# Soft-routing weights finished in one pass after attention, and three of five token tiles of each head's output normalised by ScalarE instead of VectorE

## Chip, cores and metric

One core of a Trainium2 chip. The metric is the device time of one execution in microseconds (us). The engines are TensorE (PE, matrix products; PEld is its weight load, which overlaps the products), VectorE (DVE), ScalarE (ACT), GpSimd (POOL) and SyncE (SP), which here only issues DMA transfers. Each engine runs its own instructions in the order in which they were written; semaphores order the engines among each other.

## What is computed

Three layers behind each other, in fp32: attention with a window of 128 tokens and a slope per head, a soft mixture of experts, and a feed-forward layer.

```python
scores = scale * q @ k.T                        # 4 batches x 8 heads, 576 tokens, 64 columns
scores = where(mask, scores + bias, -1e9); scores -= scores.max(-1)
attn = exp(scores); attn /= attn.sum(-1) + 1e-9
x = attn @ v                                    # 2304 tokens x 512
logits = x @ phi                                # 2304 x 32 slots
d = exp(logits - logits.max(0)); d /= d.sum(0) + 1e-9
slot_in = d.T @ x                               # 32 x 512
slot_out[e] = relu(slot_in[e] @ w1[e]) @ w2[e]  # 8 experts, 4 slots each
c = exp(logits - logits.max(1)); c /= c.sum(1) + 1e-9
y = c @ slot_out
h = y @ w_in; out = max(0.01 * h, h) @ w_out
```

Two softmaxes run over the same logits: d over the tokens (to fill the slots), and c, the combine softmax, over the 32 slots of each token.

## The kernel before

**Stages.** Attention over 32 heads g (batch g // 8), then the experts (w1, w2), then the feed-forward layer. In attention each step of a head is a small function; `UNITS` names them and `XO` gives each an offset, and step nm of head g stands at g + XO[nm]. All steps are sorted by that number and written out in that order, so a stretch of one unit holds one step of each kind, of up to five different heads. Each engine's order is what falls to it from this one list.

**A head's steps** that matter here. TQ and TK transpose Q and K (L262). HQ and HK are casts on ScalarE of the upper part of Q and K, two instructions each (L275: the Q cast writes qb, the K cast kb). LQ and LK leave the rest to kq on VectorE (L280, L282). A, B, C are scores for the row maxima (L302, into the PSUM tile sm, of which there are two), XA, XB, XC take the maxima on VectorE (L312, into mn). M transposes mn (L321), MS copies it on ScalarE (L326) and DM sends it by DMA into a row of qb (L329). S and s are the scores proper (L343, L344, the latter needs that row), E0 and E1 the exp on ScalarE (L351), G0 and G1 the masks on GpSimd, P and Q the products with V (L408) into one PSUM tile, o_ps, that all heads share. Its 65th column is the row sum. N1 adds 1e-9 (L423), N2 takes the reciprocal (L425), N3 multiplies (L429), all on VectorE, and N3 writes the head's 64 columns of xs for all five token tiles (4 of 128 tokens, one of 64). The next head's P may write o_ps only when N3 has read it.

```python
          "s": -0.3557, "E0": -0.2345, "E1": 0.1505, "G0": 0.8774, "G1": 0.979, "P": 1.0817,
          "Q": 1.1478, "N1": 1.3456, "N2": 1.5564, "N3": 1.8652}
```

N3 of head g (g + 1.8652) is followed by HQ of head g + 5 (g + 5 - 3.0925 = g + 1.9075).

**A batch's steps** (`batch_parts`, offsets in `YO`) are strewn among the heads of the next batch: transposes of xs (L452, L463) and their copies by ScalarE (L456, L466), logits (L474, added up by L495 and L502), the logits transposed (L509, L510) and copied by ScalarE to lsb (L514, L515), the maximum over the tokens (pm L519 to L523, bm L526, bmv L530, bmx L534, bt L537, btv L544), exp against it (dxv L571, dxa L578), the slots' input (sl L598, L601) and sums (ds, dsv). The combine softmax of a batch runs beside these on VectorE: maximum (tm2 L554), subtraction (tm3 L557), exp on ScalarE (tme L560), sum (cb L581), 1e-9 (cb2), reciprocal (cb3), product (cb4 L590), over the 160 logits that a partition has (5 tiles x 32 slots), into cn. For the last batch these stand in a list of their own behind attention (`TAIL`, `AFTER`).

**Behind attention** TensorE multiplies the slots' input by w1 (L823); ScalarE's Relu (L832) needs the reciprocal of the slots' sums (L828, L829). GpSimd splits cn into two fp32r parts (`csplit`, L848, L849), batches 0 and 1 before the products with w2 (L875), and TensorE transposes them (L855) after the second of these products' steps.

**Between engines on PSUM**: the framework orders any two accesses of different engines to one PSUM tile.

Of the kernel before, what the change touches and what calls it, by code (L numbers as in the profile page):

```python
# [21 lines left out]
def attn_softmoe_ffn(ctx: ExitStack, tc: tile.TileContext, q, k, v, phi, w1, w2, w_in, w_out, cst_in, out):  # L22
# [97 lines left out]
    with tc.manual_schedule():  # L120
# [22 lines left out]
        pmb = view("L", 128, 208)  # L143
        bm4 = at.tile([128, 4, 16], F32, name="bm4")
        lsb = at.tile([128, 5, NS], F32, name="lsb")
# [64 lines left out]
        nc.vector.memset(lsb[64:128, 4, :], NEG)  # L210
# [207 lines left out]
        def norm(i):  # L418
            def f(g):
# [4 lines left out]
                elif i == 1:  # L424
                    nc.vector.reciprocal(rss[g], rss[g])  # L425
                else:
                    r = rss.pop(g).unsqueeze(2)
                    for t in (slice(0, 5),) if g < NG - 1 else (slice(0, 2), slice(2, 5)):
                        nc.vector.tensor_tensor(  # L429
                            out=xs[(g // 4) % 3][:, t, g % 4 * D:g % 4 * D + D], in0=o_ps[:, t, 0:D],  # L430
                            in1=r[:, t].to_broadcast([128, t.stop - t.start, D]), op=ALU.mult)
            return f

        def batch_parts(b):
# [77 lines left out]
            def lnc():  # L512
                p = ts["ln"].rearrange("p (t s) -> p t s", t=5)
                nc.scalar.copy(out=lsb[:, 0:4, :], in_=p[:, 0:4, :])  # L514
                nc.scalar.copy(out=lsb[0:64, 4, :], in_=p[0:64, 4, :])  # L515

            def pm():
                m = small.tile([128, 1], F32, tag="pm", name="pm", bufs=1)
                nc.vector.reduce_max(out=m, in_=ts["lg"] if last else L, axis=AX.X)  # L519
                if b == 0:  # L520
                    nc.vector.tensor_copy(pmb, m.to_broadcast([128, 128]))
                else:
                    nc.vector.tensor_scalar(out=pmb, in0=m.to_broadcast([128, 128]), scalar1=mrun[(b + 1) % 2], scalar2=None, op0=ALU.max)  # L523
# [607 lines left out]
```

## Time and profile before

| | |
|---|---|
| median of 3 runs | 444.44 us (443.29 to 444.61) |
| the profiled execution | 444.21 us, its span 442.5 us |
| TensorE busy, weight loads | 427.3 us (97%), 338.4 us (76%) |
| VectorE busy | 282.9 us (64%) |
| ScalarE busy | 241.1 us (54%) |
| GpSimd busy | 119.9 us (27%) |
| attention | to about 169 us of the span |
| TensorE's granted clock | full in all 40 slices |

Busy time of TensorE counts products whose ends are modelled and which overlap, so a busy TensorE isn't one at its peak. The shares are means over stages: in attention VectorE is nearly always busy, later it is not. A step that an engine does off the chain that sets the pace costs nothing.

### The profile page before, as it was taken

Reading aid. Unit: us, or ns where it says so; the run is one execution under the profiler, and the core shown is the slowest. Engines: PE = TensorE matmul, PEld = TensorE weight load, DVE = VectorE, ACT = ScalarE, POOL = GpSimd, SP = SyncE. Lnnn points to the kernel's source line nnn. Section 1 sums busy time; section 2 is a strip of 40 time slices with the busy share of each in tenths; the row PEclk is TensorE's granted clock in tenths of the full one; section 3 lists DMA queues with packets and bytes.
Section 4 is the critical chain, followed back from the end, with each engine's and each line's share of the span. In section 5 each row is a group of like instructions: output and inputs, shape, how many; then the busy total and the mean of one; then the engine's idle time right before and its main releaser. Section 6 shows DMA issues by size and latency. Waiting matters only on the chain.

```text
span 442.5 us, 9856 instructions
## 1 busy us (share of the span) xinstructions
PE 427.3 (97%) x3490; PEld 338.4 (76%) x3490; DVE 282.9 (64%) x892; ACT 241.1 (54%) x558; POOL 119.9 (27%) x296
## 2 busy tenths in 40 slices
PE   8899998999999999999999999999999999999996
PEld 7798887788788876333776888778878888888884
DVE  5999999899999954112999776767552233225241
ACT  4587776677678733121885755555554345333330
POOL 3377667476666844020000002020202000000000
PEclk9999999999999999999999999999999999999999
DMA  7379887888978879899987005000000003003011
GB/s 168 107 227 245 227 234 218 250 219 246 237 208 232 238 222 374 291 407 412 411 293 252 7 1 190 2 1 0 1 0 0 1 0 144 0 0 145 0 73 72
DMA packets 66834, 70.30 MB, mean 159 GB/s; under 512 B 23168, under 2 KB 42016, under 8 KB 66784
## 3 DMA queue, kind: packets, MB, share of 16 engines
q1 hardware_dynamic: 66640, 69.53, 49.9%
q8 instruction: 28, 0.46, 0.5%
q14 instruction: 22, 0.18, 0.1%
q10 hardware_dynamic: 144, 0.13, 0.1%
HBM read 64.85 MB, written 4.72 MB: 157 GB/s over the span
## 4 chain that ended last, share of the span: by engine, by line
PE 85%; DVE 5%; ACT 4%; DMA 3%; issue 2%; POOL 1%; DVEq 0%; SPq 0%; ACTq 0%; POOLq 0%
PE acc L994 44%; PE o_ps L408 5%; PE sm L302 4%; PE ph L971 3%; PE st L344 3%; PE st L343 3%; DMA qb<-ms 3%; PE pb L875 3%; PE pb L823 3%; PE tp L262 3%; PE o_ps L152 2%; PE tp L452 1%; ACT kb L275 1%; PE tp L474 1%; PE tp L598 1%
## 5 line engine op out<-in xcount | busy, mean ns | idle before, releaser
L994 PE MATMUL acc<-p,p 128*128 128x512 f32 x648 | 161.3, 394 | 0.0
L994 PEld LDWEIGHTS acc<-p,p 128*128 128x128 f32 x648 | 120.3, 188 | 26.9 <-issue 2.6
L984 DVE TENSOR_TENSOR p<-ar,p 128x384 fp32r<-128x384 f32 x96 | 53.2, 556 | 92.5 <-ACT ar L980 92.3
L976 ACT ACTIVATE p<-ph 128x384 fp32r<-128x384 f32 (+1 forms) x97 | 47.5, 490 | 94.5 <-PE ph L971 94.5
L312 DVE CUSTOM_DVE_ANT_0 junk<-sm,ar 128x256 bf16<-128x256 f32 (+2 forms) x160 | 53.5, 375 | 3.0 <-PE sm L302 2.5
L994 PE MATMUL acc<-b,p 128*128 128x512 f32 x216 | 54.3, 395 | 0.0
L351 ACT ACTIVATE ar<-st 128x512 f32<-128x512 f32 x64 | 38.4, 599 | 19.2 <-PE st L344 10.4
L994 PEld LDWEIGHTS acc<-b,p 128*128 128x128 f32 x216 | 39.9, 188 | 9.8 <-issue 1.5
L980 ACT ACTIVATE ar<-ph 128x384 f32<-128x384 f32 x96 | 47.0, 489 | 0.0
L769 POOL TENSOR_TENSOR p<-ar,p 128x512 fp32r<-128x512 f32 x8 | 10.4, 1295 | 128.1 <-ACT p L769 111.4
L343 PE MATMUL st<-kq 128*128 128x256 f32 (+1 forms) x160 | 40.0, 278 | 0.0
L408 PE MATMUL o_ps<-ar 128*64 128x65 f32 x992 | 39.1, 225 | 0.0
L344 PE MATMUL st<-qb,kb 128*128 128x256 f32 (+1 forms) x160 | 36.0, 272 | 2.4 <-DMA qb<-ms 2.3
L302 PE MATMUL sm<-kb,qb 96*128 96x256 f32 (+2 forms) x160 | 34.9, 312 | 3.4 <-DVE mn L312 1.4
L408 PEld LDWEIGHTS o_ps<-ar 128*64 128x64 f32 x992 | 34.8, 138 | 4.0 <-issue 1.2
L275 ACT ACTIVATE qb<-tp 64x288 fp32r<-64x288 f32 x64 | 27.8, 434 | 9.4 <-PE tp L262 8.2
L280 DVE SCALAR_TENSOR_TENSOR kq<-tp,qb 64x288 fp32r<-64x288 f32 x64 | 29.2, 457 | 4.5 <-ACT qb L275 2.6
L971 PE MATMUL ph<-p,p 128*128 128x384 f32 x96 | 32.0, 339 | 0.0
L288 POOL TENSOR_SCALAR_AFFINE_SELECT kq<-qb 64x576 fp32r<-64x576 f32 x32 | 21.2, 662 | 37.6 <-ACT qb L275 30.6
L344 PEld LDWEIGHTS st<-qb,kb 128*128 128x128 f32 (+1 forms) x160 | 28.5, 178 | 3.6 <-DMA qb<-ms 3.5
L275 ACT ACTIVATE kb<-tp 64x288 fp32r<-64x288 f32 x64 | 27.9, 437 | 6.0 <-PE tp L262 4.6
L282 DVE TENSOR_TENSOR kq<-tp,kb 64x288 fp32r<-64x288 f32 x64 | 29.1, 455 | 1.8 <-ACT kb L275 0.2
(195 smaller groups left out, 610.4 us busy)
## 6 DMA issues: line engine op xcount, KB each, us to landing
p<-in_moe_w_dram SPq DMA_DIRECT2D x56, 256.0 KB, 4.6
p<-in_moe_w_dram SPq DMA_DIRECT2D x7, 1024.0 KB, 10.2
p<-in_moe_w_in_dram SPq DMA_DIRECT2D x5, 1024.0 KB, 5.2
p<-in_moe_w_out_dram SPq DMA_DIRECT2D x5, 1024.0 KB, 14.5
ar<-in_k_dram SPq DMA_DIRECT2D x32, 144.0 KB, 3.8
ar<-in_q_dram SPq DMA_DIRECT2D x32, 144.0 KB, 3.4
out_dram<-ar SPq DMA_DIRECT2D x17, 256.0 KB, 2.2
ar<-in_v_dram SPq DMA_DIRECT2D x32, 128.0 KB, 4.2
```

The source lines that it names most:

```text
L275: nc.scalar.activation(out=b1, in_=pr, func=AF.Copy, scale=2.0 ** (g % H - 2) if half else 1.0)
L302: nc.tensor.matmul(sl, lhsT=Q1[0:MROW, 128 * t:128 * t + mr], rhs=K1[0:MROW, c0:c1], start=True, stop=True)
L312: nc.vector.tensor_tensor_reduce(out=jk[0:mr, 0:n], in0=sl, in1=maskt[0:mr, m0:m0 + n], op0=ALU.add, op1=ALU.max, accum_out=mn[g % 2][0:mr ...
L343: nc.tensor.matmul(sl, lhsT=KX[:, k0:k1], rhs=QA[:, q0:q1], start=True, stop=False)
L344: nc.tensor.matmul(sl, lhsT=kb[g % R][:, k0:k1], rhs=qb[g % R][:, q0:q1], start=False, stop=True)
L351: nc.scalar.activation(out=e, in_=sts.pop((g, s)), func=AF.Exp, scale=2.0 ** -(g % H + 1))
L408: nc.tensor.matmul(o_ps[64 * u:64 * u + 64, t, :], lhsT=lt, rhs=r, start=st, stop=sp, tile_position=(0, 64 * u))
L971: nc.tensor.matmul(p, lhsT=mst[:, 128 * f:128 * f + 128], rhs=rhs, start=True, stop=True)
L976: nc.scalar.activation(out=G[t0, f][0][:, c], in_=H1[t0, f][:, c], func=AF.Prelu, alpha=0.01)
L980: nc.scalar.activation(out=gg, in_=H1.pop((t0, f)), func=AF.Prelu, alpha=0.01)
L984: nc.vector.tensor_tensor(out=g2, in0=G0.pop((t0, f)), in1=g1.bitcast(F32), op=ALU.subtract)
L994: nc.tensor.matmul(acc[t0][t], lhsT=(g1, g1, g2)[k][:, 128 * t:128 * t + 128], rhs=(WO1, WO2, WO1)[k][c][:, i], start=(f == f0 and k == 0) ...
```

## The change

Two things. The combine softmax leaves the batches' steps: lsb is gone, the logits are copied straight to cn, and one pass over all four batches (640 logits a partition, 20 rows of 32) follows attention, ahead of the experts' products: maximum, subtraction, exp, sum, 1e-9, reciprocal, product. And N3 does only token tiles 0 and 1 on VectorE (128 columns a partition); tiles 2, 3 and 4 are three activations on ScalarE, Copy with the reciprocal as a scale per partition, 64 columns each. The last head is as before. With it, the maximum over tokens isn't widened to 128 and 96 columns any more: the transpose reads it through a broadcast view, and the second transpose becomes four matmuls of two columns in four column groups of TensorE. No offset of a head's steps changes.

```diff
--- before
+++ after
@@ -140,9 +139,8 @@
-        pmb = view("L", 128, 208)
+        cmx = view("L", 5 * B, 208)
-        lsb = at.tile([128, 5, NS], F32, name="lsb")
@@ -207,7 +205,7 @@
-        nc.vector.memset(lsb[64:128, 4, :], NEG)
+        nc.vector.memset(cn[64:128, :, 4, :], NEG)
@@ -424,11 +422,13 @@
                 elif i == 1:
                     nc.vector.reciprocal(rss[g], rss[g])
                 else:
-                    r = rss.pop(g).unsqueeze(2)
-                    for t in (slice(0, 5),) if g < NG - 1 else (slice(0, 2), slice(2, 5)):
-                        nc.vector.tensor_tensor(
-                            out=xs[(g // 4) % 3][:, t, g % 4 * D:g % 4 * D + D], in0=o_ps[:, t, 0:D],
-                            in1=r[:, t].to_broadcast([128, t.stop - t.start, D]), op=ALU.mult)
+                    r = rss.pop(g)
+                    x = xs[(g // 4) % 3][:, :, g % 4 * D:g % 4 * D + D]
+                    for t in (slice(0, 2),) if g < NG - 1 else (slice(0, 2), slice(2, 5)):
+                        nc.vector.tensor_tensor(out=x[:, t], in0=o_ps[:, t, 0:D],
+                                                in1=r[:, t].unsqueeze(2).to_broadcast([128, t.stop - t.start, D]), op=ALU.mult)
+                    for t in (2, 3, 4) if g < NG - 1 else ():
+                        nc.scalar.activation(out=x[:, t], in_=o_ps[:, t, 0:D], func=AF.Copy, scale=r[:, t:t + 1])
             return f
 
         def batch_parts(b):
@@ -511,36 +511,32 @@
 
             def lnc():
                 p = ts["ln"].rearrange("p (t s) -> p t s", t=5)
-                nc.scalar.copy(out=lsb[:, 0:4, :], in_=p[:, 0:4, :])
-                nc.scalar.copy(out=lsb[0:64, 4, :], in_=p[0:64, 4, :])
+                nc.scalar.copy(out=cn[:, b, 0:4, :], in_=p[:, 0:4, :])
+                nc.scalar.copy(out=cn[0:64, b, 4, :], in_=p[0:64, 4, :])
 
             def pm():
-                m = small.tile([128, 1], F32, tag="pm", name="pm", bufs=1)
+                st["pm"] = m = small.tile([128, 1], F32, tag="pm", name="pm", bufs=1)
                 nc.vector.reduce_max(out=m, in_=ts["lg"] if last else L, axis=AX.X)
-                if b == 0:
-                    nc.vector.tensor_copy(pmb, m.to_broadcast([128, 128]))
-                else:
-                    nc.vector.tensor_scalar(out=pmb, in0=m.to_broadcast([128, 128]), scalar1=mrun[(b + 1) % 2], scalar2=None, op0=ALU.max)
+                if b > 0:
+                    nc.vector.tensor_tensor(out=m, in0=m, in1=mrun[(b + 1) % 2], op=ALU.max)
 
             def bm():
-                nc.tensor.transpose(tp("bm", [128, 128]), pmb, ident)
+                nc.tensor.transpose(tp("bm", [128, 128]), st["pm"].to_broadcast([128, 128]), ident)
 
             def bmv():
-                st["mx"] = mx = small.tile([128, 4, NS], F32, tag="mx", name="mx", bufs=1)
-                nc.vector.reduce_max(out=mx[:, 0, :], in_=ts.pop("bm").rearrange("p (j s) -> p s j", j=4), axis=AX.X)
-
-            def bmx():
-                mx = st["mx"]
-                nc.vector.tensor_copy(mx[:, 1:4, :], mx[:, 0:1, :].to_broadcast([128, 3, NS]))
+                st["mx"] = mx = small.tile([128, 4 * NS], F32, tag="mx", name="mx", bufs=1)[:, 0:NS]
+                nc.vector.reduce_max(out=mx, in_=ts.pop("bm").rearrange("p (j s) -> p s j", j=4), axis=AX.X)
 
             def bt():
-                nc.tensor.transpose(tp("bt", [128, 128]), st["mx"].rearrange("p a s -> p (a s)"), ident)
+                p = tp("bt", [128, 2])
+                for t in range(4):
+                    nc.tensor.matmul(p[32 * t:32 * t + 32, :], lhsT=st["mx"], rhs=ident[:, 0:2], start=True, stop=True, tile_position=(0, 32 * t))
 
             def btv():
                 mo, mw = mrun[(b + 1) % 2], mrun[b % 2]
                 p = ts.pop("bt")
                 if b > 0:
-                    st["al"] = al = small.tile([128, 1], F32, tag="al", name="al", bufs=1)
+                    st["al"] = al = small.tile([128, 16], F32, tag="al", name="al", bufs=1)[:, 0:1]
                     nc.vector.tensor_tensor(out=al, in0=mo, in1=p[:, 0:1], op=ALU.subtract)
                 if not last:
                     nc.vector.tensor_copy(mw, p[:, 0:1])
@@ -548,16 +544,6 @@
             def bta():
                 if b > 0:
                     nc.scalar.activation(out=st["al"], in_=st["al"], func=AF.Exp)
-
-            def tm2():
-                st["cm"] = m = small.tile([128, 5], F32, tag="cm", name="cm", bufs=1)
-                nc.vector.reduce_max(out=m, in_=lsb, axis=AX.X)
-
-            def tm3():
-                nc.vector.tensor_tensor(out=cn[:, b], in0=lsb, in1=st["cm"].unsqueeze(2).to_broadcast([128, 5, NS]), op=ALU.subtract)
-
-            def tme():
-                nc.scalar.activation(out=cn[:, b], in_=cn[:, b], func=AF.Exp)
 
             dq = [(slice(0, 128), slice(0, 4)), (slice(0, 64), slice(4, 5))]
 
@@ -566,9 +552,9 @@
-                        nc.vector.tensor_tensor(out=dn[r, t], in0=p[r, t], in1=st["mx"][r, 0:1, :].to_broadcast([r.stop, t.stop - t.start, NS]), op=ALU.subtract)
+                        nc.vector.tensor_tensor(out=dn[r, t], in0=p[r, t], in1=st["mx"][r].unsqueeze(1).to_broadcast([r.stop, t.stop - t.start, NS]), op=ALU.subtract)
-                    nc.vector.tensor_tensor(out=dn, in0=lsb, in1=st["mx"][:, 0:1, :].to_broadcast([128, 5, NS]), op=ALU.subtract)
+                    nc.vector.tensor_tensor(out=dn, in0=cn[:, b], in1=st["mx"].unsqueeze(1).to_broadcast([128, 5, NS]), op=ALU.subtract)
@@ -576,18 +562,6 @@
                         nc.scalar.activation(out=st["dn"][r, t], in_=st["dn"][r, t], func=AF.Exp)
                 else:
                     nc.scalar.activation(out=st["dn"], in_=st["dn"], func=AF.Exp)
-
-            def cb():
-                nc.vector.reduce_sum(out=st["cm"], in_=cn[:, b], axis=AX.X)
-
-            def cb2():
-                nc.vector.tensor_scalar(out=st["cm"], in0=st["cm"], scalar1=1e-9, scalar2=None, op0=ALU.add)
-
-            def cb3():
-                nc.vector.reciprocal(st["cm"], st["cm"])
-
-            def cb4():
-                nc.vector.tensor_tensor(out=cn[:, b], in0=cn[:, b], in1=st["cm"].unsqueeze(2).to_broadcast([128, 5, NS]), op=ALU.mult)
 
             def sl():
                 p, dn = tp("sl", [128, 512], "st"), st["dn"]
...
@@ -794,8 +763,15 @@
             for i in range(n):
                 nc.tensor.matmul(t[:, 0:128], lhsT=ident, rhs=ident, start=True, stop=True)
 
-        for k in AFTER:
-            after[k]()
+        cf = cn.rearrange("p b t s -> p (b t) s")
+        cmb = cmx.unsqueeze(2).to_broadcast([128, 5 * B, NS])
+        nc.vector.reduce_max(out=cmx, in_=cf, axis=AX.X)
+        nc.vector.tensor_tensor(out=cf, in0=cf, in1=cmb, op=ALU.subtract)
+        nc.scalar.activation(out=cf, in_=cf, func=AF.Exp)
+        nc.vector.reduce_sum(out=cmx, in_=cf, axis=AX.X)
+        nc.vector.tensor_scalar(out=cmx, in0=cmx, scalar1=1e-9, scalar2=None, op0=ALU.add)
+        nc.vector.reciprocal(cmx, cmx)
+        nc.vector.tensor_tensor(out=cf, in0=cf, in1=cmb, op=ALU.mult)
         he, so = ar[:, x0:x0 + F], ar[:, x0 + F:x0 + F + DM]
 
         def to_hT(h):
```

The order in which ScalarE does its work, before, from the sum of the logits' first half (L495) over the next two heads (kb, qb: casts of K and Q of a head; st: scores; ms: maxima; tp: a transpose in PSUM):

```order
L495 COPY ar<-tp 128x144
L275 ACTIVATE kb_88<-tp 64x288 x2
L351 ACTIVATE ar<-st 128x512
L326 CAST ms<-tp 5x128
L456 COPY ar<-tp 128x4x128
L351 ACTIVATE ar<-st 128x512
L275 ACTIVATE qb_92<-tp 64x288 x2
L275 ACTIVATE kb_91<-tp 64x288 x2
```

And in the changed kernel, the same place:

```order
L495 COPY ar<-tp 128x144
L273 ACTIVATE kb_88<-tp 64x288 x2
L349 ACTIVATE ar<-st 128x512
L324 CAST ms<-tp 5x128
L456 COPY ar<-tp 128x4x128
L349 ACTIVATE ar<-st 128x512
L431 ACTIVATE ar<-o_ps,rs 128x64 x3
L273 ACTIVATE qb_92<-tp 64x288 x2
L273 ACTIVATE kb_91<-tp 64x288 x2
```

The three activations (L431) stand between the exp and the next Q cast; so they do in every head, but for one in eight in which a copy of a transpose (L456) comes between them and the cast. The first of them waits for VectorE's piece of the same normalisation, which stands ahead of it in the program.

VectorE's order, before, in the head that holds the middle of a batch's steps (dn: exponents of the slots' softmax; mx: maxima over tokens; cm: the combine softmax's rows; rs: row sums):

```order
L280 SCALAR_TENSOR_TENSOR kq_96<-tp,qb_95 64x288 x2
L571 TENSOR_TENSOR dn<-lsb,mx 128x160
L534 COPY mx<-mx 128x96
L282 TENSOR_TENSOR kq_96<-tp,kb_94 64x288 x2
L423 TENSOR_SCALAR rs<-o_ps 128x5
L312 ISA junk,mn_99<-sm,ar 64x192
L312 ISA mn_99 64x1
L425 RECIPROCAL rs<-rs 128x5
L554 TENSOR_REDUCE cm<-lsb 128x5
L557 TENSOR_TENSOR cn<-lsb,cm 128x160
L544 TENSOR_TENSOR al<-col,tp 128x1
L546 COPY col<-tp 128x1
```

And in the changed kernel:

```order
L557 TENSOR_TENSOR dn<-cn,mx 128x160
L280 TENSOR_TENSOR kq_96<-tp,kb_94 64x288 x2
L421 TENSOR_SCALAR rs<-o_ps 128x5
L310 ISA junk,mn_99<-sm,ar 64x192
L310 ISA mn_99 64x1
L423 RECIPROCAL rs<-rs 128x5
L540 TENSOR_TENSOR al<-col,tp 128x1
L542 COPY col<-tp 128x1
L428 TENSOR_TENSOR ar<-o_ps,rs 128x2x64
```

The widening copy and the two steps of the combine softmax are gone from between the rest of K and the normalisation, and that is two token tiles wide.

VectorE's order at the end of attention in the changed kernel (col: the slots' sums; pa: a product in PSUM), where before the same steps were 160 wide and of the last batch alone:

```order
L598 TENSOR_TENSOR col<-col,tp 32x1
L768 TENSOR_REDUCE ar<-cn 128x20
L769 TENSOR_TENSOR cn<-cn,ar 128x640
L771 TENSOR_REDUCE ar<-cn 128x20
L772 TENSOR_SCALAR ar<-ar 128x20
L773 RECIPROCAL ar<-ar 128x20
L774 TENSOR_TENSOR cn<-cn,ar 128x640
L804 TENSOR_SCALAR col<-pa 128x1
L805 RECIPROCAL col<-col 128x1
```

The reciprocal for the Relu (L804, L805) stands behind the whole pass.

## Rows read from the trace of the kernel before

**Rows 1.** Busy time of each engine in a stretch of attention (count), clock, DMA.
```profile
30.00:150.00 120.00, 115.37 (x1584) 99.75 (x1583) 112.35 (x467) 86.33 (x208) 78.94 (x206) 1.00 0.86 233
```
**Rows 2.** TensorE's waits in 30 to 150: in total, times, longest.
```profile
PEld sm L302 <- ACT kb L275: 3.7, 12, 0.4
PEld st L344 <- DMA qb<-ms: 3.5, 5, 1.7
...
PEld sm L302 <- DVE mn L312: 1.2, 4, 0.6
```
**Rows 3.** Timeline of ScalarE: start, duration, what, [idle before and its releaser].
```profile
90.89 0.88 ACT L275 ACTIVATE kb<-tp 64x288 fp32r<-64x288 f32 x2
...
93.34 0.59 ACT L456 COPY ar<-tp 128x512 f32<-128x512 f32 x1 [0.81 <-PE tp L452]
93.82 0.60 ACT L351 ACTIVATE ar<-st 128x512 f32<-128x512 f32 x1
94.31 0.89 ACT L275 ACTIVATE qb<-tp 64x288 fp32r<-64x288 f32 x2
95.22 0.89 ACT L275 ACTIVATE kb<-tp 64x288 fp32r<-64x288 f32 x2
...
98.10 0.91 ACT L275 ACTIVATE qb<-tp 64x288 fp32r<-64x288 f32 x2 [0.19 <-PE tp L262]
```
**Rows 4.** Timeline of VectorE in the same heads.
```profile
95.58 0.94 DVE L280 SCALAR_TENSOR_TENSOR kq<-tp,qb 64x288 fp32r<-64x288 f32 x2
96.56 0.94 DVE L282 TENSOR_TENSOR kq<-tp,kb 64x288 fp32r<-64x288 f32 x2
...
98.09 0.49 DVE L429 TENSOR_TENSOR ar<-o_ps,rs 128x320 f32<-128x320 f32 x1
...
99.86 0.94 DVE L280 SCALAR_TENSOR_TENSOR kq<-tp,qb 64x288 fp32r<-64x288 f32 x2
```
**Rows 5.** L429, the normalisation: ns shortest/median/longest, first and last start, shapes.
```profile
L429 DVE TENSOR_TENSOR ar<-o_ps,rs x31: 472/490/493, 26.8 to 167.2; 128x320 f32<-128x320 f32 x31
L429 DVE TENSOR_TENSOR ar<-ol,rs x2: 291/318/345, 168.8 to 169.0; 128x128 f32<-128x128 f32 x1, 128x192 f32<-128x192 f32 x1
```
**Rows 6.** Timeline of ScalarE: two neighbouring copies of different width.
```profile
108.33 0.27 ACT L514 COPY lsb<-tp 128x128 f32<-128x128 f32 x1
108.49 0.18 ACT L515 COPY lsb<-tp 64x32 f32<-64x32 f32 x1
```
**Rows 7.** Timeline of ScalarE: the first Relu of the experts.
```profile
184.44 0.69 ACT L832 ACTIVATE ar<-pb,col 128x512 f32<-128x512 f32 x1 [6.69 <-PE pb L823]
```
**Rows 8.** Timeline at the tail: a copy of the logits and its wait.
```profile
171.48 0.28 ACT L500 COPY ar<-tp 128x144 f32<-128x144 f32 x1 [0.88 <-DVE pm L519]
```
**Rows 9.** Timeline of ScalarE: casts and a copy of the other heads.
```profile
86.12 0.88 ACT L275 ACTIVATE kb<-tp 64x288 fp32r<-64x288 f32 x2
...
89.81 0.43 ACT L275 ACTIVATE qb<-tp 64x288 fp32r<-64x288 f32 x1 [1.01 <-PE tp L262]
...
102.80 0.59 ACT L456 COPY ar<-tp 128x512 f32<-128x512 f32 x1 [0.67 <-PE tp L452]
...
107.41 0.89 ACT L275 ACTIVATE qb<-tp 64x288 fp32r<-64x288 f32 x2 [0.18 <-PE tp L262]
...
111.61 0.88 ACT L275 ACTIVATE qb<-tp 64x288 fp32r<-64x288 f32 x2 [0.29 <-PE tp L262]
...
119.28 0.88 ACT L275 ACTIVATE kb<-tp 64x288 fp32r<-64x288 f32 x2 [1.74 <-PE tp L262]
...
123.75 0.88 ACT L275 ACTIVATE qb<-tp 64x288 fp32r<-64x288 f32 x2
```
**Rows 10.** Busy time of what touches cm, 30 to 168: VectorE (count), clock, DMA.
```profile
30.00:168.00 138.00, 5.67 (x18) 1.00 0.84 233
```
**Rows 11.** Timeline behind attention: VectorE's reduction, GpSimd's first split after transposes.
```profile
176.72 0.30 DVE L554 TENSOR_REDUCE cm<-lsb 128x5 f32<-128x160 f32 x1
...
194.54 0.32 POOL L848 CAST ar<-cn 128x160 fp32r<-128x160 f32 x1 [17.55 <-PE pa L855]
```

More of the change, by code (lines that the diff above doesn't have):

```diff
@@ L48, in attn_softmoe_ffn @@
           "xs": 9.4718, "xsc": 9.7691, "lh": 10.0639, "lgc": 10.0708, "pm": 10.6372, "lx": 10.7576,
-          "bm": 11.6027, "bmv": 11.8446, "ln": 10.8721, "lnc": 10.9955, "bmx": 12.1976, "dxv": 12.0436,
+          "bm": 11.6027, "bmv": 11.8446, "ln": 10.8721, "lnc": 10.9955, "dxv": 12.0436,
           "dxa": 12.5969, "bt": 12.663, "btv": 12.7744, "bta": 12.9593, "sl": 12.8123, "slv": 13.1223,
-          "ds": 13.3756, "dsv": 13.7379, "tm2": 12.6955, "tme": 13.0753, "cb": 13.9763, "tm3": 12.7455,
-          "cb2": 13.9963, "cb3": 14.0163, "cb4": 14.0363}
+          "ds": 13.3756, "dsv": 13.7379}
     ZA = {"DQK": 0.8, "DV": 1.2, "W0": 0.3, "EARLY": 0.8, "L0": 3.0, "L1": 4.0,
@@ L624, in dsv @@
                 nc.vector.tensor_tensor(out=ssum[0:NS], in0=ssum[0:NS], in1=p[0:NS, 2:3], op=ALU.add)
-            F.update(lgc=lgc, lx=lx, ln=ln, lnc=lnc, pm=pm, bm=bm, bmv=bmv, bmx=bmx, bt=bt, btv=btv, bta=bta, tm2=tm2, tme=tme,
-                     dxv=dxv, dxa=dxa, tm3=tm3, cb=cb, cb2=cb2, cb3=cb3, cb4=cb4, sl=sl, slv=slv, ds=ds, dsv=dsv)
+            F.update(lgc=lgc, lx=lx, ln=ln, lnc=lnc, pm=pm, bm=bm, bmv=bmv, bt=bt, btv=btv, bta=bta,
+                     dxv=dxv, dxa=dxa, sl=sl, slv=slv, ds=ds, dsv=dsv)
             return F
@@ L633, in attn_softmoe_ffn @@
                  "G0": mask(0), "G1": mask(1), "P": attend(0), "Q": attend(1), "N1": norm(0), "N2": norm(1), "N3": norm(2)}
-        TAIL = ["xt3", "xt5", "xt4", "xt3c", "xt5c", "xt4c", "lh", "pm", "lgc", "lx", "bm", "ln", "bmv", "dxv", "dxa", "bmx", "bt", "sl",
-                "btv", "bta", "lnc", "slv", "ds", "dsv", "tm2", "tm3"]
+        TAIL = ["xt3", "xt5", "xt4", "xt3c", "xt5c", "xt4c", "lh", "pm", "lgc", "lx", "bm", "ln", "bmv", "dxv", "dxa", "bt", "sl",
+                "btv", "bta", "lnc", "slv", "ds", "dsv"]
         TAIL = [(B - 1, nm) for nm in TAIL]
-        AFTER = [(B - 1, nm) for nm in ("tme", "cb", "cb2", "cb3", "cb4")]
         LAST = {"xt2": 5.07, "xs": 5.1, "xt2c": 5.3, "xsc": 5.31, "li": 6.3}
         FILL = dict(zip(("xt4", "lh", "ln", "bt", "ds"), WN[2:]))
-        after = {}
         ev = []
@@ L646, in attn_softmoe_ffn @@
             for nm, f in batch_parts(b).items():
-                if (b, nm) in AFTER:
-                    after[b, nm] = f
-                    continue
                 if (b, nm) in TAIL:
```

## The prediction

> **What bounds the kernel now.** I read the busy times of the attention stage first, then what TensorE waited for there, then the engines' timelines head by head, and last the start of the expert stage. Between 30 and 150 us TensorE is busy 115.37 of 120 us and VectorE 112.35, while ScalarE has 86.33 [rows 1]. So TensorE stands idle for 4.63 us at most, and whatever makes VectorE lighter can return no more than that in this stretch; ScalarE looks as if it had 33 us to give away. The waits say otherwise: TensorE's weight loads for the row-max scores (L302) waited for the K cast of ScalarE (L275) 12 times, 3.7 us, for the row of maxima coming by DMA 3.5 us, and for VectorE's maxima only 1.2 us [rows 2]. ScalarE has idle time, but not where TensorE waits for it.
>
> The timeline shows the tie. In one head the K cast ends at 91.77, TensorE then does scores and a transpose, ScalarE copies that transpose at 93.34 after a wait of 0.81 us for it, and from there runs without a gap: exp at 93.82, Q cast at 94.31, K cast at 95.22 until 96.11 [rows 3]. That is a closed ring of 4.34 us (K cast, TensorE, copy, exp, Q cast, K cast); anything put between exp and Q cast lengthens it. VectorE has a ring of its own in these heads: its rest of Q starts at 95.58 and again at 99.86, 4.28 us with no gap [rows 4].
>
> **The change, part by part.**
>
> *VectorE's share of the normalisation.* It falls from 320 columns a partition (490 ns) to 128; the last head has such a piece, 291 ns [rows 5]. That is 0.20 us off VectorE in 30 heads, 6 us of VectorE's time. None of it shortens a ring that I found closed on TensorE; it helps where TensorE waits for maxima, and the bound on that is the 1.2 us of [rows 2]. I credit the whole 1.2.
>
> *ScalarE's share.* Three activations of 64 columns with a scale per partition. Nothing like it is in the trace. A 64x32 copy takes 0.18 us and a 128x128 one 0.27, and the second of them starts 0.16 after the first, so neighbours overlap by 0.11 [rows 6]; 64 columns lie at some 0.21. A Relu with a scale per partition takes 0.69 at 512 columns [rows 7], against 0.60 for an exp with a plain scale [rows 3]: 0.09 for the scale. One is 0.30 then, three in a row hold the engine 3 x (0.30 - 0.11) = 0.57, say 0.6. Below: the scale's 0.09 vanishes in the overlap, 3 x 0.10 = 0.3. Above: no overlap, as the two halves of a Q cast show none (0.89 for the two [rows 3], 0.43 for one [rows 9]), 3 x 0.30 = 0.9. I take 0.6, by the overlapping rows, since these are neighbours with separate columns.
> By itself: the Trainium skill, page "ScalarE: Activation LUTs", section "What ACT_TABLE_LOAD costs", gives 186 ns + 0.833 ns per column, 93 ns more for a pointer operand, and an overlap of 93 ns; that would be some 0.72 us for the three (an estimate), and by it the time below would be about 2 us more. The same page's rules for kernel authors put multiplications on VectorE rather than ScalarE.
>
> *When they may start.* The built order puts the three after the exp and ahead of the next Q cast, and the Q cast can't pass them. They need the reciprocal, and they also come behind VectorE's piece: both read one PSUM tile, and the trace shows that two engines that only read one are kept apart, for ScalarE's copy at 171.48 waited 0.88 us for VectorE's maximum over the same tile, although it needs nothing of it [rows 8]. By itself: the Trainium skill, page "PSUM — Partial Sum Buffer", section "PSUM bank collisions raise a hardware error", says reads against reads of one bank count as collisions; the trace agrees that they are ordered. So a normalisation on ScalarE starts no earlier than: K cast's end, 0.03, then from VectorE's rest of K to its normalisation (96.56 to 98.09) 1.53, its piece 0.29, a semaphore 0.04 [rows 4, 5]: 1.89 us after the K cast, 1.93 where the rest of Q is still running.
>
> *What that does in eight heads of one batch*, each with its Q cast [rows 3, 9]:
> - 89.81: ScalarE had waited 1.01 us for TensorE; the K cast ended at 87.00, so the three run from 88.93 to 89.53. Nothing lost.
> - 94.31: no gap in the ring. All of 0.6 lost.
> - 98.10: start at 96.11 + 1.93 = 98.04, Q cast at 98.64, 0.54 late, of which I let TensorE's other work take 0.15: 0.4.
> - 103.28: the three stand ahead of a copy that waits 0.67 us for TensorE. Nothing.
> - 107.41: VectorE also does the batch's logits and maximum in front, so by the same count the start is at about 107.5 and the cast 0.7 late, less TensorE's own work: 0.5.
> - 111.61: the cast had waited 0.29 us for TensorE, which covers part; 0.4 late by the same count, less TensorE's own work: 0.15.
> - 116.59: the K cast behind it waits 1.74 us for TensorE anyway. Nothing.
> - 123.75: directly behind the copy. 0.6.
>
> That is 2.25 us in a batch of eight. At 0.3 the same list gives 0.3 + 0.1 + 0.2 + 0 + 0.3 = 0.9, at 0.9 it gives 3.8. By the offsets, the normalisation of head g stands ahead of the Q cast of head g + 5, so 27 of the 31 have a cast behind them: 3.4 batches, 7.6 us (3.0 to 12.8). Against it stand the 1.2 us of maxima, and the DMA's 3.5 us [rows 2]: longer heads give that transfer more time, and I credit half, 1.75 (bounds 0 and all).
>
> *Combine softmax in attention.* Reductions, subtractions, reciprocal and product on the tile cm take VectorE 5.67 us between 30 and 168 [rows 10]; three batches' worth goes, with the copies that widened maxima. The heads where they stood (Q casts at 89.81, 116.59, 123.75) are the ones whose pace TensorE sets, so I put nothing more on it. The ScalarE exp that goes stood in the head of 123.75, where ScalarE waits for TensorE after it. The replaced transpose (four small matmuls in four column groups instead of one) I put at nothing: the same weight columns, in a head that has room.
>
> *The single pass behind attention.* VectorE's reduction over 160 elements takes 0.30 us [rows 11]; four times as many at about one a nanosecond is 0.8. Two reductions, subtraction, product, exp on ScalarE and two small ones are some 4.6 us from 176.8: done at about 181.4. Behind it on VectorE is the reciprocal of the slot sums, which the Relu at 184.44 needs: that Relu waited 6.69 us for TensorE [rows 7], so some 2.5 us are left. GpSimd's splits of batches 0 and 1 follow, eight operations of which the shorter take 0.32 us; the transposes that need them were done by 194.54, 13 us after the pass [rows 11]. The cover is TensorE's expert matmuls; without it the pass would cost its whole 4.6 us. In the tail the widened maximum and its copy shorten a chain by 0.2 us.
>
> **Sum.** 7.6 - 1.2 - 1.75 - 0.2 = 4.45 us more. The profiled execution took 444.21 us (span 442.5), the runs' median is 444.44, so no correction is worth making: 444.2 + 4.4 = **448.6 us**, 1.0% slower. With the bounds: 3.0 - 1.2 - 3.5 - 0.2 = -1.9 (442.3) to 12.8 - 0.4 = 12.4 (456.6). A measurement of this kernel can't tell 0.3% (1.3 us) from no change.
>
> **Rivals.**
> *VectorE is the bound* (ends on the other side). For it: 94% busy, and periods of 4.28 us without a gap [rows 1, 4]. Then 0.20 us a head and the combine work come off the pace, and TensorE's idle time is the limit: at most 4.63 us, 439.6; I would expect half to all of it, 439.6 to 442. Against it: TensorE names VectorE for only 1.2 us of waits. It decides if the three activations fit into ScalarE's gaps, that is, if they take 0.3 us rather than 0.6 and VectorE's earlier finish starts them sooner than I have it.
> *The two cancel*: cheap activations, most DMA waits gone: within 1.3 us of 444.3.
> *The activations are dear*: 0.9 us, no overlap, no DMA credit: 452 to 457. For it: the casts' lack of overlap.
> *The pass behind attention shows.* If it took 7.3 us or more, the Relu at 184.44 would be late by the excess; from the rows that is 2.5 us off, and I give it 3%, adding 1 to 3 us.
>
> **Chances.** The forecast's mechanism with 0.4 to 0.75 us each, 446 to 452: 45%. Dear activations: 14%. Pass: 3%, counted as slower. Cancel: 14%. VectorE bound: 24%. Slower by over 0.3%: 0.61; within: 0.15; faster: 0.24. The likeliest case has 446 to 452 for itself; with both signs the range is 440 to 455, which leaves out the far ends of the VectorE case and of the dear one.
>
> **What the profile after would show.** Right: 93 activations of 128x64 of some 0.3 us, the first of each three waiting for VectorE's piece; the Q cast directly behind the third; TensorE's waits for the K cast above 3.7 us and for the DMA below 3.5; heads of about 5.1 us against 4.85 (89.81 to 123.75, seven heads); the expert stage shifted, not changed, with the Relu still waiting for TensorE. Wrong: heads at or below 4.7 us with VectorE idle, or Q casts that still wait for TensorE after the three, which would make VectorE the engine that set the pace.

## The result and the profile after

450.72 us (median of 4 runs, 449.90 to 452.09), beside 443.98 for the kernel before on the same chip: ratio 1.0148, 95% interval 1.0114 to 1.0183. The change makes the kernel 1.5% slower. The profiled execution took 449.90 us, span 448.2, against 444.21 and 442.5: 5.7 us more.

Busy time in the same stretch as [rows 1], the changed kernel:

```profile
30.00:150.00 120.00, 110.94 (x1547) 96.16 (x1545) 99.87 (x436) 97.08 (x270) 76.06 (x198) 1.00 0.81 225
```

VectorE, 112.35 before, is down to 99.87, ScalarE is up from 86.33 to 97.08, and TensorE, which should have profited, does less in the same 120 us: 110.94 instead of 115.37, 37 products fewer. The clock is full in both. So TensorE waits more, although the engine that looked full was relieved.

Waits in 30 to 154 us of the changed kernel (in total, times, longest), in answer to [rows 2]:

```profile
PEld sm L300 <- ACT kb L273: 7.6, 20, 0.6
DVE kq L278 <- ACT qb L273: 7.9, 19, 0.7
DVE junk L310 <- PE sm L300: 7.5, 13, 0.9
PEld o_ps L406 <- issue: 5.3, 10, 0.7
PEld o_ps L406 <- POOL ar L367: 3.7, 9, 0.5
PE o_ps L406 <- issue: 3.6, 7, 0.6
PE sm L300 <- ACT kb L273: 3.4, 17, 0.4
ACT ar L431 <- DVE ar L428: 1.3, 3, 0.6
```

The wait for the K cast has doubled: 7.6 us, where the kernel before has 3.9 in the same window (3.7 up to 150 us). VectorE, where it had no gap in its ring [rows 4], now waits for the Q cast (7.9) and for scores (7.5, before 1.5). Waits in front of the product with V (L406), 0.8 us before, have grown too. What is gone are the two waits that [rows 2] had beside the K cast: those for the DMA and for VectorE's maxima have no row any more.

The normalisation's two parts (ns shortest/median/longest, first and last start, shape):

```profile
L431 ACT ACTIVATE ar<-o_ps,rs x93: 303/314/335, 26.6 to 173.5; 128x64 f32<-128x64 f32 x93
```
```profile
L428 DVE TENSOR_TENSOR ar<-o_ps,rs x31: 271/291/294, 26.3 to 172.7; 128x128 f32<-128x128 f32 x31
```

The ring of [rows 3], ScalarE's timeline in the same two heads, now 1.0 to 2.1 us later, and behind them the head of 107.41:

```profile
94.37 0.59 ACT L456 COPY ar<-tp 128x512 f32<-128x512 f32 x1 [0.80 <-PE tp L452]
94.85 0.60 ACT L349 ACTIVATE ar<-st 128x512 f32<-128x512 f32 x1
95.34 0.73 ACT L431 ACTIVATE ar<-o_ps,rs 128x64 f32<-128x64 f32 x3
95.93 0.88 ACT L273 ACTIVATE qb<-tp 64x288 fp32r<-64x288 f32 x2
96.83 0.88 ACT L273 ACTIVATE kb<-tp 64x288 fp32r<-64x288 f32 x2
...
99.64 0.72 ACT L431 ACTIVATE ar<-o_ps,rs 128x64 f32<-128x64 f32 x3
100.24 0.86 ACT L273 ACTIVATE qb<-tp 64x288 fp32r<-64x288 f32 x2
...
109.52 0.72 ACT L431 ACTIVATE ar<-o_ps,rs 128x64 f32<-128x64 f32 x3 [0.58 <-DVE ar L428]
110.12 0.88 ACT L273 ACTIVATE qb<-tp 64x288 fp32r<-64x288 f32 x2
```

The copy still waits 0.80 us for TensorE, as before; between exp and Q cast 0.59 us are new, and from the copy to the K cast's end ScalarE runs without a gap. TensorE's side of it:

```profile
96.17 1.23 PE L406 MATMUL o_ps<-ar 128*64 128x65 f32 x32 [0.46 <-issue]
...
97.76 0.56 PE L300 MATMUL sm<-kb,qb 96*64 96x192 f32 x3 [0.15 <-ACT kb L273]
```

The product with V starts 0.10 us after the end of the third activation (95.34 + 0.73 = 96.07), whose reads of o_ps it has to let pass; the scores then wait for the later K cast. In 19 of the 30 heads that have such a product next, it starts 0.09 to 0.11 us after the third activation's end, whatever releaser its row names. And in 21 of the 31 heads the first activation starts 0.03 to 0.06 us after VectorE's piece of the same head ends; in the closed head of 98.10 (99.64 above) that costs ScalarE 0.13 us of standing idle, too short for the list of waits.

**Head by head.** The starts of the Q casts in ScalarE's timelines give the time by which each comes later, measured from the cast before it (so no head is charged for an earlier one). For the eight heads of the prediction's list, worked out from the casts' starts in each kernel's profile; the second column is the prediction's, the others are measured, less the same head before:

```
Q cast (before)  forecast  after   e1     e3     e9    e10    e11
  89.81           0       -0.02   0.00  -0.06  -0.02   0.01  -0.02
  94.31           0.6      0.59   0.00   0.71   0.57   0.00   0.58
  98.10           0.4      0.52   0.02   0.38   0.53  -0.03   0.53
 103.28           0       -0.30   0.97  -0.25  -0.29   0.14  -0.31
 107.41           0.5      0.87  -0.11   0.28   0.41  -0.14   0.88
 111.61           0.15     0.32   0.01   0.23   0.46   0.34   0.31
 116.59           0        0.18  -0.18   0.10  -0.09   0.45  -0.50
 123.75           0.6     -0.28   0.00  -0.02  -0.02  -0.89   0.40
 sum              2.25     1.88   0.71   1.37   1.55  -0.12   1.87
```

(e1 to e11 are the experiments below.) The last Q cast comes at 155.06 instead of 150.48, 4.6 us later; the last normalisation ends attention 5.5 us later. The 0.9 between them is a wait of its own, to which the last experiment comes.

**Behind attention.** The single pass, VectorE and then ScalarE:

```profile
182.04 0.80 DVE L768 TENSOR_REDUCE ar<-cn 128x20 f32<-128x640 f32 x1
182.88 0.82 DVE L769 TENSOR_TENSOR cn<-cn,ar 128x640 f32<-128x640 f32 x1
184.56 0.82 DVE L771 TENSOR_REDUCE ar<-cn 128x20 f32<-128x640 f32 x1 [0.86 <-ACT cn L770]
...
185.94 0.83 DVE L774 TENSOR_TENSOR cn<-cn,ar 128x640 f32<-128x640 f32 x1
...
186.87 0.17 DVE L805 RECIPROCAL col<-col 128x1 f32<-128x1 f32 x1
```
```profile
183.79 0.74 ACT L770 ACTIVATE cn<-cn 128x640 f32<-128x640 f32 x1 [1.24 <-DVE cn L769]
190.20 0.69 ACT L808 ACTIVATE ar<-pb,col 128x512 f32<-128x512 f32 x1 [5.67 <-PE pb L799]
```

From 182.04 to 186.77 it takes 4.73 us. The Relu's reciprocal is there at 187.04 and the Relu at 190.20 waits for TensorE, as in [rows 7], 5.76 us later than before. That is attention's loss carried on; between the reciprocal and the Relu 3.2 us are left.

### The profile page after: what moved, and what is told of

Read it like the earlier page. It is cut to its first block, busy times and chain, and to the rows that moved or that the text cites. A ratio compares the mean times of both kernels' runs of the same rounds, so it can differ in the third digit from the quotient of the medians.

```text
span 448.2 us, 9953 instructions
## 1 busy us (share of the span) xinstructions
PE 425.4 (95%) x3518; PEld 336.4 (75%) x3518; DVE 273.2 (61%) x869; ACT 259.2 (58%) x648; POOL 119.8 (27%) x296
## 4 chain that ended last, share of the span: by engine, by line
PE 79%; ACT 6%; POOL 6%; issue 4%; DVE 2%; DMA 1%; SPq 0%; DVEq 0%; ACTq 0%; POOLq 0%
PE acc L970 43%; PE o_ps L406 6%; PE ph L947 3%; PE pb L799 3%; PE pb L851 3%; PE sm L300 3%; PE st L341 3%; ACT kb L273 2%; PE st L342 2%; PE tp L260 2%; POOL kq L286 2%; PE tp L452 1%; POOL ar L357 1%; ACT qb L273 1%; PE tp L572 1%
## 5 line engine op out<-in xcount | busy, mean ns | idle before, releaser
L406 PE MATMUL o_ps<-ar 128*64 128x65 f32 x992 | 38.6, 224 | 7.6 <-issue 3.8
L406 PEld LDWEIGHTS o_ps<-ar 128*64 128x64 f32 x992 | 34.8, 138 | 12.3 <-issue 5.5
L300 PEld LDWEIGHTS sm<-kb,qb 96*128 96x128 f32 (+1 forms) x160 | 21.7, 179 | 10.7 <-ACT kb L273 9.9
L341 PEld LDWEIGHTS st<-kq 128*128 128x128 f32 (+1 forms) x160 | 28.6, 178 | 1.4 <-issue 0.9
```

Source lines behind the costliest of these rows:

```text
L300: nc.tensor.matmul(sl, lhsT=Q1[0:MROW, 128 * t:128 * t + mr], rhs=K1[0:MROW, c0:c1], start=True, stop=True)
L341: nc.tensor.matmul(sl, lhsT=KX[:, k0:k1], rhs=QA[:, q0:q1], start=True, stop=False)
L406: nc.tensor.matmul(o_ps[64 * u:64 * u + 64, t, :], lhsT=lt, rhs=r, start=st, stop=sp, tile_position=(0, 64 * u))
```

## The experiments

Ratios are against the kernel before on the same chip.

**e1: one part alone, the combine softmax.** N3 as before, on VectorE for all tiles; the rest as changed.

```diff
-                    for t in (slice(0, 2),) if g < NG - 1 else (slice(0, 2), slice(2, 5)):
+                    for t in (slice(0, 5),) if g < NG - 1 else (slice(0, 2), slice(2, 5)):
...
-                    for t in (2, 3, 4) if g < NG - 1 else ():
-                        nc.scalar.activation(out=x[:, t], in_=o_ps[:, t, 0:D], func=AF.Copy, scale=r[:, t:t + 1])
```

> Only the combine softmax moves behind attention; VectorE normalises all five token tiles as before. If ScalarE's place in the ring of casts is the cause of the whole loss, this part alone is worth little: 443.0 to 444.2 us, ratio 0.997 to 1.000, TensorE's waits for the K cast in 30 to 150 us as before (about 3.7 us). If VectorE sets the pace of attention, taking some 6 us of work from it shows: 441.5 us or less. If the pass behind attention shows, it is slower than before, 445 us or more.

443.29 us, ratio 0.9993 (0.9974 to 1.0012): nothing. Busy in 30 to 150 us:

```profile
30.00:150.00 120.00, 115.33 (x1599) 99.91 (x1598) 108.29 (x449) 85.85 (x206) 78.69 (x206) 1.00 0.83 232
```

VectorE has 4 us less to do and TensorE is as busy as before to 0.04 us. Less work for VectorE alone returns nothing.

**e2: the other part alone.** The kernel before with N3 split as in the change; the combine softmax stays among the heads.

> Only the normalisation is split (two tiles VectorE, three ScalarE); the combine softmax stays among the heads. If the three activations in the ring are the cause: nearly the whole loss of the changed kernel or more, 450 to 452.5 us, ratio 1.013 to 1.02. If the loss came from the pass behind attention or from the broadcast and the four small matmuls, this one is near before, 443 to 446 us.

452.39 us, 1.0202 (1.0168 to 1.0236). The whole loss belongs to the split, and more than that: with the combine steps still in VectorE's way the three activations waited 4.9 us for its piece between 30 and 154 us (7 times, up to 1.0), against 1.3 in the changed kernel. So the first half of the change is worth some 2 us, but only as a repair of the second; the two ratios' intervals just overlap (1.0168 and 1.0183), so the 2 us are rough.

**e3: ScalarE's time without its waits.** e1, and in each head three activations of 128x64 with a scale per partition where the change has them, which read a constant and write a scratch tile that nobody uses.

```diff
+        dmy = at.tile([128, 2, D], F32, name="dmy")
...
+                    for t in (2, 3, 4) if g < NG - 1 else ():
+                        nc.scalar.activation(out=dmy[:, t % 2], in_=ident[:, 0:D], func=AF.Copy, scale=ones[:, 0:1])
```

> As the run with the combine part alone, VectorE normalising all five tiles, with three additional activations of 128x64 in each head at the place where the changed kernel has its three; they read constants, write a scratch tile, and nothing waits for them or for PSUM. If ScalarE's time in the ring is the cause: within 1.5 us of the changed kernel, 449 to 451 us. If the cause is what the real ones wait for (VectorE's piece, the reciprocal) or what waits for them (the next product with V on the shared PSUM tile): near the run with the combine part alone, 443 to 446 us.

447.81 us, 1.0095 (1.0067 to 1.0122): between the two forecasts, and neither of them came true. Three activations that wait for nothing and for which nobody waits cost 0.95% of the 1.48%. They are a little longer (from SBUF 338 ns, and the cast starts 0.72 us after the first instead of 0.59), so this is no less than the share of ScalarE's time.

```profile
95.40 0.82 ACT L432 ACTIVATE dmy<-ident,col 128x64 f32<-128x64 f32 x3
96.12 0.88 ACT L274 ACTIVATE qb<-tp 64x288 fp32r<-64x288 f32 x2
```

In the closed head of 94.31 each kind costs the time for which it holds ScalarE: 0.71 here, 0.59 in the changed kernel. In that of 98.10 the real ones cost 0.14 more (0.52 against 0.38), because they start behind VectorE's piece; that the two heads together come out alike, 1.09 against 1.11, is chance. The largest cost beyond ScalarE's time is in the head of 107.41 (0.87 against 0.28), where the activation of 109.52 waits for VectorE, and at the end of attention (e12).

**e4: ScalarE's three ahead of VectorE's piece**, by writing the two loops in the other order.

> The changed kernel with the order of the two parts of a normalisation turned: ScalarE's three activations first, VectorE's two tiles behind them. If the ring's length is the three activations themselves: little, 449.5 to 451 us, the start of the three earlier by up to 0.33 us in the few heads that waited for VectorE's piece. If waiting behind VectorE's piece is what costs: 3 us less, about 447.5 us. Against it, VectorE's piece now waits for ScalarE and holds the maxima behind it by up to 0.6 us a head: then slower than the changed kernel.

456.83 us, 1.0296 (1.0267 to 1.0326). The wait only changes sides, and hits VectorE. Waits in 30 to 154 us:

```profile
DVE ar L430 <- ACT ar L428: 22.7, 24, 2.4
...
PE o_ps L406 <- DVE ar L430: 8.1, 11, 0.9
```

Two readers of one PSUM tile stand behind each other, whichever is first; with ScalarE first, VectorE's maxima stand behind the activations too.

**e5: one tile instead of three on ScalarE**, `(slice(0, 4),)` and `(4,)` in the two loops.

> The changed kernel with only token tile 4 on ScalarE (one activation), tiles 0 to 3 on VectorE. If the loss is made of the time that the activations hold ScalarE in the ring (0.20 us each) and of a start that waits for VectorE's piece: the hold falls from 0.60 to 0.20 us, the start is 0.13 us later, so about 2 to 3.5 us over before, 446 to 447.5 us. If a fixed cost of having ScalarE take part is the larger share (the wait for VectorE's piece, the product waiting for two engines), it stays near the changed kernel: 449 us or more.

446.93 us, 1.0067 (1.0043 to 1.0091), as expected. A third of the activations, 45% of the loss.

**e6: the three activations behind the Q cast**, as a step N4 of their own at 1.92, ahead of the K cast.

> The changed kernel with the three activations moved behind the Q cast instead of ahead of it (between Q cast and K cast), so that the Q cast never waits for VectorE's piece. They still hold ScalarE for 0.6 us in the same ring, ahead of the K cast. If waiting for VectorE's piece is the share that the dummy activations lacked: like those, 447 to 449 us. If the product with V, which may write the shared PSUM tile only behind the three, is that share, this is worse than the changed kernel, as the three end 0.9 us later: 453 us or more.

465.95 us, 1.0493 (1.0459 to 1.0527), the worst of all. One head of it, TensorE, ScalarE and GpSimd:

```profile
100.24 1.23 PE L406 MATMUL o_ps<-ar 128*64 128x65 f32 x32 [1.42 <-POOL kq L286]
```
```profile
98.34 0.86 ACT L273 ACTIVATE qb<-tp 64x288 fp32r<-64x288 f32 x2 [1.00 <-PE tp L260]
99.23 0.28 ACT L499 COPY ar<-tp 128x144 f32<-128x144 f32 x1
99.41 0.73 ACT L423 ACTIVATE ar<-o_ps,rs 128x64 f32<-128x64 f32 x3
```
```profile
99.28 0.66 POOL L286 TENSOR_SCALAR_AFFINE_SELECT kq<-qb 64x576 fp32r<-64x576 f32 x1 [1.64 <-ACT qb L273]
```

The row puts TensorE's 1.42 us down to GpSimd, but that operation ended at 99.94. The third activation ended at 100.14, and TensorE started 0.10 later, the same 0.10 as in the changed kernel: it waits for ScalarE to have read o_ps. The tile that all heads share makes a late normalisation a late product with V.

**e7 and e8: ScalarE unloaded elsewhere.** The copy of a batch's transposes (L456) given to VectorE, one a batch on top of e1 (e7), two a batch on top of the change (e8, the diff; e7 has `kc == 1`).

```diff
-                xt(f"xt{kc}", kc, 0, 4, nc.scalar.copy)
+                xt(f"xt{kc}", kc, 0, 4, nc.vector.tensor_copy if kc > 0 and not last else nc.scalar.copy)
```

> The run with the combine part alone, and one copy of a batch's transposes (xt1c, the one behind which the Q cast of each eighth head stands without a gap) on VectorE instead of ScalarE. The ring of that head loses 0.49 us on ScalarE if VectorE, lighter there without the combine softmax, takes the copy in time: 1 to 1.7 us in all, 441.6 to 442.7 us. If VectorE sets the pace: no gain or a loss, 443 us or more.

> The changed kernel with the copies of two transposes of each batch (xt1c, xt2c) on VectorE instead of ScalarE: in the two heads where the ring has no gap, ScalarE gives back 0.49 us of the 0.6 that the three activations took. Ring theory: 2.5 to 4 us less than the changed kernel, 446.5 to 448.5 us. If ScalarE's time in these heads isn't what counts: 449.5 to 452 us.

444.58 (1.001, 0.9992 to 1.0028) and 452.88 (1.0182, 1.0149 to 1.0214): both forecasts of a gain missed. e7 came out where its text had put VectorE as the bound, e8 just above the range for ScalarE's time not being what counts. The traces show why that doesn't follow. In e7 the three heads with the copy on VectorE (44.95, 85.22, 123.75) are 0.43 to 0.95 us shorter than in e1, so ScalarE's time does count there, and the head behind each is 0.39 to 0.45 longer. In the last of them VectorE waits 1.12 us for TensorE's transposes, copies from 122.20, then normalises, and the product with V waits for that:

```profile
123.44 1.23 PE L406 MATMUL o_ps<-ar 128*64 128x65 f32 x32 [0.50 <-DVE ar L427]
```

In e8 the copy comes between VectorE's reciprocal and its piece, and the activations, which need both, wait with it (VectorE, then ScalarE):

```profile
96.95 0.69 DVE L456 COPY ar<-tp 128x512 f32<-128x512 f32 x1
97.56 0.28 DVE L428 TENSOR_TENSOR ar<-o_ps,rs 128x128 f32<-128x128 f32 x1
```
```profile
97.87 0.72 ACT L431 ACTIVATE ar<-o_ps,rs 128x64 f32<-128x64 f32 x3 [0.68 <-DVE ar L428]
```

Work taken off a ring through one engine came back as a wait for the other.

**e9: VectorE's piece earlier.** Three of a batch's steps (pm, bmv, btv) moved from just ahead of N3 to just behind it.

```diff
-"pm": 10.6372
+"pm": 10.8655
...
-"bmv": 11.8446
+"bmv": 11.8655
...
-"btv": 12.7744
+"btv": 12.8655
```

> The changed kernel, with three of a batch's steps on VectorE (logits' maximum, maximum after its transpose, and the column of maxima) moved from just ahead of the normalisation to just behind it. Theory A (two parts: the three activations hold ScalarE 0.6 us in closed rings, and in some heads they also wait for VectorE's piece behind these steps): the heads with the batch's steps lose 0.3 to 0.6 less, three batches, so 1 to 1.7 us less than the change: 449.0 to 449.7. Rival B (only ScalarE's own time counts): 450.7, unchanged. Rival C (the steps themselves are on the path of the batch's softmax, so that moving them later costs): above 451.

449.52 us, 1.0123 (1.0098 to 1.0149). Where it was aimed it did what was expected: in the head of 107.41 the activations start 2.11 us after the K cast's end (107.62 to 109.73) instead of 2.58 (106.94 to 109.52), and the loss falls from 0.87 to 0.41. Its like in the two other batches go from 0.58 to 0.53 and from 0.35 to -0.10; of the heads behind the three, two lose 0.14 us more than in the change.

```profile
109.41 0.29 DVE L428 TENSOR_TENSOR ar<-o_ps,rs 128x128 f32<-128x128 f32 x1
109.62 0.29 DVE L519 TENSOR_REDUCE pm<-ar 128x1 f32<-128x144 f32 x1
```
```profile
109.73 0.72 ACT L431 ACTIVATE ar<-o_ps,rs 128x64 f32<-128x64 f32 x3
```

The total lies 1.2 us under the change's, but the two intervals overlap, and in the profiled execution an early head (44.95), where TensorE waited 0.67 us for the row of maxima by DMA, took 0.71 longer than in the change, so that its span is only 0.4 shorter. The place is shown, the gain in total isn't.

**e10 and e11: the split in some heads only.** e10 splits where the list expects no loss (12 heads: the Q casts of 89.81, 103.28, 116.59 and their like), e11 in the others (19).

```diff
+                    on = g < NG - 1 and g % 8 in (0, 3, 5)
...
-                    for t in (2, 3, 4) if g < NG - 1 else ():
+                    for t in (2, 3, 4) if on else ():
```

> The changed kernel, with the split normalisation only in heads g with g % 8 in 0, 3, 5, the three whose Q cast the prediction's list puts at a loss of nothing; the other heads are normalised by VectorE alone. Theory A (the cost depends on whether the head's ring through ScalarE is closed): as the combine softmax alone, 443.3 to 444.3. Rival B (a fixed cost for each split head, 7.4 us over 31): 12 heads x 0.24 = 2.9 us, 446.2. Rival C (VectorE's relief is a gain where ScalarE has room): below 443.

> The complement: the split normalisation only in the heads with g % 8 in 1, 2, 4, 6, 7. Theory A: nearly the whole loss stays, or a little more, as no head gives back: 449.5 to 452. Rival B (fixed cost for each split head): 19 heads x 0.24 = 4.6 us, 447.9.

e10: 443.25 us, 0.9996 (0.9973 to 1.0019); e11: 449.78, 1.0131 (1.0106 to 1.0156). Twelve split heads cost nothing (0.8 us at most by the interval), the other nineteen nearly all; a fixed cost for each split head (446.2 and 447.9) lies outside both intervals. A head of e10, ScalarE:

```profile
101.22 0.72 ACT L432 ACTIVATE ar<-o_ps,rs 128x64 f32<-128x64 f32 x3 [0.45 <-DVE ar L429]
101.82 0.59 ACT L457 COPY ar<-tp 128x512 f32<-128x512 f32 x1
102.29 0.89 ACT L273 ACTIVATE qb<-tp 64x288 fp32r<-64x288 f32 x2
```

The copy had waited 0.67 us for TensorE [rows 9] and now has no wait: the activations sit in that gap. The price isn't that of an activation, but that of an activation in a closed ring. And relief of VectorE in 12 heads is worth nothing even there.

**e12: one head, number 28, whole on VectorE.** TensorE in the changed kernel, near attention's end:

```profile
164.34 0.65 PE L452 MATMUL tp<-ident,ar 128*128 128x128 f32 x4
...
166.34 1.23 PE L406 MATMUL o_ps<-ar 128*64 128x65 f32 x32 [1.35 <-POOL ar L360]
```

Before, this product followed the transposes at once. Now it needs the three activations, which stand behind an exp and the copy of those same transposes and end at 166.25.

> The changed kernel, with one head of the 31, number 28, normalised by VectorE alone. In the changed kernel TensorE stands idle for 1.35 us ahead of the product with V at 166.34, behind that head's three activations, which stand behind an exp and a copy that itself waits for a transpose. Theory A (this one wait is a loss of its own, which no Q cast shows): 1.4 us less than the change, attention's end 1.3 to 1.5 us earlier, 449.0 to 449.5. Rival B (the wait only takes the place of another; a head is worth its share of the loss): 0.2 us less, 450.5.

449.73 us, 1.0122 (1.0085 to 1.0158). The wait is gone:

```profile
165.59 0.66 PE L453 MATMUL tp<-ident,ar 128*128 128x128 f32 x4
166.17 1.26 PE L406 MATMUL o_ps<-ar 128*64 128x65 f32 x32
```

From the copy of the transposes to the second exp behind it 1.94 us pass, against 3.33 in the changed kernel, so this one head cost 1.4. The total fell by 1.0, with overlapping intervals; the profiled span fell only 0.2, since in that execution three early heads (40.04, 44.95, 54.09), whose code is the change's, took 0.9 longer.

## Why the prediction was right, and where it was off

- **What bounds the kernel.** Right as far as the change goes: ScalarE between TensorE's results and TensorE's needs, not VectorE, which looked full at 94%. e1 and e10 take work off VectorE and get nothing; e3 adds work to ScalarE alone and finds two thirds of the loss. The rival of VectorE as the bound (439.6 to 442) is out. That ScalarE alone is the bound isn't shown: VectorE's ring of 4.28 us is as long as ScalarE's 4.34, and e7, which takes 0.49 us off ScalarE in one head of eight but puts 0.69 on VectorE, gains nothing.
- **ScalarE's share, 0.6 us a head.** Right: from the first activation to the Q cast 0.59 to 0.60, one 314 ns instead of 0.30. The Trainium skill, page "ScalarE: Activation LUTs", section "What ACT_TABLE_LOAD costs", would give some 0.72 (an estimate) by its 186 ns, 93 per pointer operand, 0.833 per column and 93 of overlap; the trace disagrees for the three that read PSUM and agrees for those of e3 that read SBUF.
- **The list of heads.** 2.25 forecast, 1.88 measured for this batch; the seven heads from 90.84 to 126.68 take 5.12 us on average, 5.1 forecast. The earliest start came as put: 1.93 us behind the K cast in the head of 98.10. Two heads of no loss (89.81, 103.28) and the closed ones came as forecast (94.31: 0.59, 98.10: 0.52); 116.59 lost 0.18 and 111.61 0.32, twice its 0.15. The head of 107.41 was mis-sized, 0.87 instead of 0.5: I let TensorE's other work cover 0.2 that nothing covered, and the activations started at 2.58 after the K cast rather than 2.4 (e9 shows that the batch's maximum ahead of VectorE's piece does it). The head of 123.75 was put at 0.6 and gained 0.28: from its K cast to its Q cast it did lose 0.62 (4.47 to 5.09), but that K cast comes 0.90 sooner behind the Q cast before it (2.69 to 1.79), as its wait of 1.74 for TensorE [rows 9] shrinks to 0.84. With the dummies of e3 it shrinks too (1.93), in e1 it doesn't (2.70); why, no run isolates. Over all 27 casts, the heads that got longer add up to 8.0 us, against 7.6.
- **The credits.** 2.95 forecast (maxima 1.2, DMA 1.75); the heads that got shorter give back 2.9, but not where I put it. Two heads (72.12 and 78.26) give 1.5 (0.44 and 1.04), where TensorE had waited for the DMA; but e1 and e7, in which no head is longer by the split, have the same two shorter by 2.4 and 2.1 together, so how much of it the longer heads gave isn't shown. Four others, that of 103.28 among them, give 1.1 (0.11 to 0.40 each), for which I had nothing. That the sum fits is luck; e1's single heads move by 0.97 and more without the total moving. The 1.2 of the maxima had the wrong cause: I credited VectorE's lighter normalisation, but in e3, where VectorE normalises all five tiles, those waits are gone as well, and so are the DMA's, while e1 keeps both (1.4 and 3.8 us in 30 to 154). So the waits go when heads get longer, with or without a lighter normalisation on VectorE.
- **Off: "27 of the 31 have a cast behind them".** That step was wrong: I charged heads only through a late Q cast and let the last four cost nothing. One cost 1.4 us through the product with V, a wait that stood in no term of the sum (e12). With 0.5 given back beside it, attention ends 5.5 us later instead of 4.6.
- **The combine softmax** in attention: nothing, right (e1); with the split it saves some 2 us of waiting (e2), which the list had in it without saying so, since its starts were read from heads in which those steps would be gone or elsewhere. **The pass**: 4.73 us for 4.6, hidden, as forecast. The tail's credit of 0.2 did not appear: attention's end to the Relu takes 0.25 more.
- **The sum.** +4.45 forecast against the profiled execution, +5.7 measured: 8.0 lost and 2.9 given back among the casts, less 0.5 by which this execution was ahead at its first Q cast already, 0.9 behind the last cast and 0.25 in the tail. The difference from the forecast is mainly the head at the end. Two slips change little: the split is in 31 heads, not 30, and the upper sum takes off 0.4 that no term explains; by its own terms it is 12.8 - 1.2 - 0.2 = 11.4 (455.6). The median of the runs lies another 0.8 above the profiled execution, which makes 450.7.

What stays open: how the remaining loss splits between ScalarE's time and waits for VectorE's piece to better than about 1 us, since single executions of the same code differ by 0.9 us in early heads.

## What to carry to other kernels

An engine that is idle 28% of a stretch, as ScalarE was here, has time to give only where its idle time lies: before moving work to it, find the ring through it and the engine that waits (copy, exp, cast, TensorE), and count heads one by one; the same 0.6 us of work cost nothing in twelve heads and 5.8 of the 6.7 us in nineteen. Where the accesses of two engines to one PSUM tile are ordered, as here, they read it one behind the other, and the next writer waits for the later one (e4, e6), so a split adds a wait at both ends. And a step without the consumer one has in mind has another: look for who writes the buffer next.

## What the hardware showed unexpectedly

An activation of 128x64 with a scale per partition takes 314 ns from PSUM and, in e3, 338 ns from SBUF, and three in a row hold ScalarE 0.59 to 0.60 us there and 0.72 here. Both write SBUF, so I put the difference down to the source, which no run tested by itself. And the releaser that the trace names for a wait on several semaphores was off by 0.20 us in e6: the engine that ended last was another.
